# Block one's last pair first, low words on VectorE and MLP rows that run on, in a kernel of top-32 attention and two MLPs

## The chip, the cores and the metric

The kernel runs on one core of a Trainium2 chip. The metric is the device time of one execution in microseconds (us). A core has five engines with a queue of instructions each: TensorE (PE in the rows; PEld is its weight load), VectorE (DVE), ScalarE (ACT), GpSimd (POOL) and SyncE (SP), which here only issues DMAs.

## What is computed

q, k and v are 4 batches x 8 heads x 576 positions x 64, all float32. Each row of scores keeps its 32 largest entries; the rest is masked away before the softmax. The 4 x 576 = 2304 rows of the result (8 x 64 = 512 wide) go through two MLPs of 512 -> 2048 -> 512.

```python
scores = scale * np.matmul(q, k.transpose(0, 1, 3, 2))
kth = np.partition(scores, -32, axis=-1)[..., -32:-31]
scores = np.where(scores >= kth, scores, -1e9)
attn = softmax(scores)                   # sum + 1e-9
x = concat_heads(np.matmul(attn, v))     # 2304 x 512
h = np.maximum(x @ w_in, 0);  x = (h * h) @ w_out
h = x @ w2_in;  out = np.maximum(0.01 * h, h) @ w2_out
```

The MLPs' weights reach the chip as 64-bit floats and are turned there into two words each, a high and a low one, both in the matmul's reduced float32 format; the same is done with q, k, x and the hidden layer. A product then takes three matmuls (high by high, high by low, low by high).

## The kernel before

**Attention.** A tile is 128 rows of scores x 576 columns, of one pair of heads. Two tiles make a pair; there are 72 pairs. `UNITS` orders the rows: unit 0 and 1 are rows 0 to 511 of batch 0, unit 2 is rows 0 to 255 of batch 1, unit 3 the last 64 rows of batch 0, unit 4 the last 320 of batch 1, and units 5 to 8 are batches 2 and 3. For each unit the four head pairs come one after another. VectorE finds the 32 largest of a tile in four rounds: MAX8 gives the 8 largest, MATCH_REPLACE8 strikes them out (lines 867 and 869). Then, for a pair: `shifts` (L315, GpSimd) takes threshold minus maximum, `drop` (L321) and `expo_sum` (L325) are ScalarE's masking and exponential with the sum, `recip` (L329 on GpSimd, L330 on VectorE) the reciprocal, `pt_main` (L339) transposes on TensorE into a PSUM bank of the three called `att`. `pt_left` does the last 64 columns and transposes the reciprocal. For units 0 and 1 the transposed tile is kept as float32 (`PT`, L349), `av` (L425) multiplies by V and `x_out` scales by the reciprocal (`xn`, L456). For units from 2 on (`split`, tiles 32 and up) the exponentials are scaled beforehand (`norm`) and the transposed tile is split in two words: ScalarE copies the bank twice, once as the high word (`PTs`, L344) and once whole (`whole`, L346), and GpSimd subtracts (L347). `x_out` then writes the two words of x (`xh` L457, `xl` L460) into the buffers of the MLP.

**Scores ahead.** Batches 2 and 3 (`EARLY`) have their scores computed long before they are searched: `scores` (L303, L304) into `stage` and out to DRAM, read back later by `load_s`. These `fill` events lie in slots 2 to 245 (`FILL`). The unit called `KEPT` (unit 3) is treated so too, beside unit 1 whose K it shares.

**The MLPs.** x is cut in six blocks of 512, 256, 384, 512, 256 and 384 rows; units 0 and 1 are block one (index 0), unit 2 is block two, units 3 and 4 block three. A block goes through layer one in 16 steps of 128 hidden units (h matmuls L619, acc matmuls L656), then through layer two (L619, L656 and L658). The 32 steps of block one are the first use of the weights. For each, a DMA brings 1 MB of 64-bit words, `w_convert` makes the two-word weights (ScalarE L532 and L541, VectorE's bit operations L547 and L548, ScalarE's high part L552, GpSimd's subtraction L553) and `w_store` writes 1 MB to DRAM, from which later blocks load them. In the first step of a layer the chunks of x are taken in the order `OPENING`, so that it can start before the last head pair is there.

**What sets the order.** The program is written out in slots; pair p has slots 16p to 16p+15, one search operation each, and `at(slot, f)` puts everything else at a slot before or after (scores 30 before, shift 14 after the pair's first slot, transposes at 20, `av` at 30). `run_moe` emits MLP work between: per slot `rate` quanta of three matmuls. A block's rate is its quanta by the slots until the next block is ready (L824), and when a block becomes ready what is left of the one before is emitted at once (the `while active` under L875). A scheduler then orders each engine's queue by priority (order of writing, with attention 100 ahead, `SOON`) and by a model of times; `issue_after` pins an instruction behind another. Block one is ready at slot 274 (16 x 15 + 30 + 4, for its last pair is pair 15), block two at slot 402.

The lines that pace the MLP and convert the first two weight steps:

```python
rate.append(sum(quanta(*ph) for ph in groups[j]) / max(nxt - rslot[j] - 1, 40))   # L824
at(rslot[0] - 80, w_raw, 0)
at(rslot[0] - 28, convert_now, 0)
at(rslot[0] - 14, convert_now, 1)
```

Of the kernel before, what the change touches and what calls it, by code (L numbers as in the profile page):

```python
# [8 lines left out]
F = mybir.dt.float32  # L9
R = mybir.dt.float32r  # L10
U = mybir.dt.uint32
# [34 lines left out]

KEPT = 3

EARLY = (2, 3)
FILL = (2, 245)  # L50
KPB = 2
NST = 5
SDB = 2
SPB = 3

NS = 6
# [8 lines left out]

SOON = 100
SEAM = 400
CONVP = 30

# [17 lines left out]
def topk_attention_moe_moe2_kernel(  # L87
# [127 lines left out]
    def at(slot, fn, *a):  # L215
        events.setdefault(slot, []).append((fn, a))


    KT = {}
# [65 lines left out]
    def scores(t, half):  # L285
# [50 lines left out]
    def pt_main(t):  # L336
        ps = bank()
        for j in range(NJ):
            PE.transpose(ps[:, j * P:(j + 1) * P], t["e"][:, j * P:(j + 1) * P], ident)  # L339
        c = t["col"]  # L340
        x = ps.rearrange("p (j t) -> p j t", j=NJ)
        if split(t["uh"]):
            pts = late["PT"]
            ACT.activation(pts[:, 0:4, c:c + P], x, AF.Copy)  # L344
            whole = late["pool"].tile([P, NJ, P], F, tag="whole", name="whole", bufs=2)
            ACT.activation(whole, x, AF.Copy)  # L346
            POOL.tensor_tensor(pts[:, 4:8, c:c + P], whole, pts.bitcast(F)[:, 0:4, c:c + P], op=OP.subtract)  # L347
        else:
            ACT.activation(PT[:, 0:4, c:c + P], x, AF.Copy)  # L349
# [94 lines left out]
    def x_out(uh, hs):  # L444
# [13 lines left out]
        if m < n:  # L458
            ACT.activation(spill[r, hp, 0:n - m], x[r, m:n], AF.Copy)
        POOL.tensor_tensor(xl[r, c:c + m], x[r, 0:m], xh.bitcast(F)[r, c:c + m],  # L460
                                                   op=OP.subtract)
        if hp == NHP - 1 and hs[-1] == 1 and g0 + n >= end:
# [62 lines left out]
    def w_convert_steps(i):  # L525
# [30 lines left out]
        for todo in STAGES:  # L556
            for fn, x in todo:
                dict(high=high, bits=bits, parts=parts)[fn](x)
            yield 0

    def w_store(i):
# [206 lines left out]

    pairs = []
    for p in range(NPAIRS):  # L770
        pr = dict(t=tiles[2 * p:2 * p + 2], p=p)
        pairs.append(pr)
        z = 16 * p
        for i, t in enumerate(pr["t"]):
            if kept(t["uh"]):
# [25 lines left out]
    for uh in uhs:  # L801
        if split(uh):
# [6 lines left out]
            continue  # L809
        apart = uh["n"] > P and uh["n"] % P and uh["ti"] % 2 == 0  # L810
        for hs in ((0,), (1,)) if apart else ((0, 1),):
            z = 16 * (uh["lastA"] // 2 if hs == (0,) else uh["last"] // 2) + 30
            nq = 2 * len(hs)
            for i in range(nq):
                at(z + i, av, uh, hs, i)
            at(z + nq, x_out, uh, hs)
# [4 lines left out]
    rate = []  # L821
    for j, blk in enumerate(blocks):
        nxt = rslot[j + 1] if j + 1 < len(blocks) else rslot[j] + 40
        rate.append(sum(quanta(*ph) for ph in groups[j]) / max(nxt - rslot[j] - 1, 40))  # L824

    def convert_now(i):
        for _ in w_convert(i):
            pass

    at(rslot[0] - 80, w_raw, 0)  # L830
    at(rslot[0] - 80, w_raw, 1)
    at(rslot[0] - 28, convert_now, 0)
    at(rslot[0] - 27, w_raw, 2)
    at(rslot[0] - 14, convert_now, 1)
    at(rslot[0] - 13, w_raw, 3)
    at(rslot[0] - 10, w_store, 0)

# [3 lines left out]
    def run_moe(amount):  # L841
        while amount >= 1 and active:
            try:
                next(active[0])
                amount -= 1
            except StopIteration:
                active.pop(0)
        return amount
# [3 lines left out]
    while slot <= last:  # L852
# [20 lines left out]
        for fn, a in events.pop(slot, []):  # L873
            nr = len(ready)
            with tc.high_priority(offset=SOON):  # L875
                fn(*a)
            for blk in ready[nr:]:
                if not (len(ready) > nr + 1 and blk is ready[-1]):
                    while active:
                        run_moe(1)  # L880
                if blk["idx"] + 1 < len(blocks) and blocks[blk["idx"] + 1].get("spilled"):
                    unspill(blocks[blk["idx"] + 1])
                active.extend(moe(*ph) for ph in groups[blk["idx"]])
                credit = 0.0
                cur["rate"] = rate[blk["idx"]]
        if active:
# [56 lines left out]
```

## Time and profile before

| what | us |
|---|---|
| median of 3 runs (lowest, highest) | 1193.88 (1189.94, 1194.23) |
| the profiled execution | 1189.77 |
| its span, first to last instruction | 1188.0 |
| TensorE busy / VectorE / ScalarE / GpSimd | 1124.0 / 872.1 / 820.1 / 744.8 |
| a load of raw weights, 1 MB, issue to landing (32 of them) | 7.9 |
| a store of converted weights, 512 KB (64 of them) | 7.8 to 8.4 |

The profile is of one execution. Times in the rows are from the span's start. Busy times of the engines overlap, so they don't add up to the span. An engine's own idle time costs only where the end waits for it. The matmuls' ends are modelled, so the time from one matmul's start to the next is a better measure of pace than a single duration.

### The profile page before, as it was taken

Reading aid. Unit: us, or ns where it says so; the run is one execution under the profiler, and the core shown is the slowest. Engines: PE = TensorE matmul, PEld = TensorE weight load, DVE = VectorE, ACT = ScalarE, POOL = GpSimd, SP = SyncE. Lnnn points to the kernel's source line nnn. Section 1 sums busy time; section 2 is a strip of 40 time slices with the busy share of each in tenths; the row PEclk is TensorE's granted clock in tenths of the full one; section 3 lists DMA queues with packets and bytes.
Section 4 is the critical chain, followed back from the end, with each engine's and each line's share of the span. In section 5 each row is a group of like instructions: output and inputs, shape, how many; then the busy total and the mean of one; then the engine's idle time right before and its main releaser. Section 6 shows DMA issues by size and latency. Waiting matters only on the chain.

```text
span 1188.0 us, 20096 instructions
## 1 busy us (share of the span) xinstructions
PE 1124.0 (95%) x6376; PEld 985.5 (83%) x6376; DVE 872.1 (73%) x1828; ACT 820.1 (69%) x1823; POOL 744.8 (63%) x958
## 2 busy tenths in 40 slices
PE   5899977989899999999999999999999999999997
PEld 4777765868688899898998998788888899998996
DVE  7999999888886668999999999989997400110010
ACT  6999998899989667887676777556766743332322
POOL 7968846999879677677886775767665653002100
PEclk9999989999899999999999999999999999999999
DMA  9868756899999698799888888667776499779973
GB/s 307 287 216 276 264 187 230 312 334 333 394 353 360 199 336 293 240 346 371 312 264 296 286 283 287 217 219 219 232 234 215 151 326 334 256 252 351 346 258 119
DMA packets 108201, 329.53 MB, mean 277 GB/s; under 512 B 17216, under 2 KB 25408, under 8 KB 104000
## 3 DMA queue, kind: packets, MB, share of 16 engines
q1 hardware_dynamic: 105472, 323.53, 79.8%
q10 hardware_dynamic: 2624, 4.72, 1.1%
q8 instruction: 52, 0.85, 0.3%
q14 instruction: 53, 0.43, 0.1%
HBM read 257.03 MB, written 71.17 MB: 276 GB/s over the span
## 4 chain that ended last, share of the span: by engine, by line
PE 57%; DVE 21%; ACT 12%; DMA 5%; issue 2%; POOL 2%; ACTq 0%; SPq 0%; POOLq 0%; DVEq 0%
PE h L619 22%; PE acc L658 13%; DVE m L867 10%; PE acc L656 9%; DVE w L869 8%; PE att L425 3%; PE att L436 3%; PE att L339 3%; ACT e L321 2%; ACT stage L304 1%; PE sp L303 1%; ACT e L325 1%; DMA wraw<-in_w_dram 1%; DMA out_dram<-y 1%; ACT s L304 1%
## 5 line engine op out<-in xcount | busy, mean ns | idle before, releaser
L619 PE MATMUL h<-xh,wi 128*128 128x512 f32 (+2 forms) x1280 | 345.9, 344 | 9.7 <-ACT ga L629 4.5
L867 DVE MAX8 m<-w 128x8 f32<-128x576 f32 x432 | 315.1, 756 | 1.8
L619 PEld LDWEIGHTS h<-xh,wi 128*128 128x128 f32 x1280 | 225.4, 190 | 38.6 <-ACT ga L629 6.7
L639 POOL TENSOR_TENSOR gl<-ga,gh 128x512 fp32r<-128x512 f32 (+2 forms) x160 | 162.5, 1018 | 137.2 <-ACT gh L638 110.9
L869 DVE MATCH_REPLACE8 w<-m,w 128x576 f32<-128x576 f32 x288 | 215.2, 751 | 0.5
L619 PE MATMUL h<-xl,wi 128*128 128x512 f32 (+2 forms) x640 | 203.3, 338 | 0.0
L347 POOL TENSOR_TENSOR PTs<-whole,PTs 128x512 fp32r<-128x512 f32 x112 | 144.6, 1297 | 43.7 <-ACT whole L346 43.2
L656 PE MATMUL acc<-gh,wo 128*128 128x512 f32 (+2 forms) x768 | 156.5, 343 | 0.8 <-ACT y L674 0.5
L658 PE MATMUL acc<-wo,gh 128*128 128x512 f32 x576 | 152.1, 396 | 0.5 <-ACT gh L638 0.5
L656 PEld LDWEIGHTS acc<-gh,wo 128*128 128x128 f32 x768 | 127.4, 190 | 13.4 <-ACT y L674 0.7
L321 ACT ACTIVATE e<-s,m 128x576 f32<-128x576 f32 x144 | 112.9, 785 | 32.3 <-DVE m L867 27.4
L639 DVE TENSOR_TENSOR gl<-ga,gh 128x384 fp32r<-128x384 f32 x32 | 17.9, 559 | 152.1 <-ACT gh L638 149.4
L619 PEld LDWEIGHTS h<-xl,wi 128*128 128x128 f32 x640 | 120.0, 189 | 10.6
L636 ACT ACTIVATE ga<-h 128x512 f32<-128x512 f32 (+2 forms) x96 | 46.6, 491 | 116.3 <-PE h L619 114.8
L658 PEld LDWEIGHTS acc<-wo,gh 128*128 128x128 f32 x576 | 105.4, 188 | 21.2 <-ACT gh L638 0.9
L867 DVE MAX8 m<-s 128x8 f32<-128x576 f32 x144 | 104.3, 754 | 17.7 <-ACT s L304 15.2
L325 ACT ACTIVATE e<-e,nb 128x576 f32<-128x576 f32 x144 | 111.5, 782 | 1.8 <-POOL nb L315 1.7
L869 DVE MATCH_REPLACE8 w<-m,s 128x576 f32<-128x576 f32 x144 | 108.2, 752 | 0.6
L339 PE MATMUL att<-ident,e 128*128 128x128 f32 x576 | 90.1, 277 | 7.6 <-DVE wc L548 3.0
L334 POOL TENSOR_SCALAR e<-e,rc 128x576 f32<-128x576 f32 x112 | 82.5, 748 | 16.0 <-DVE rc L330 14.5
L656 PE MATMUL acc<-gl,wo 128*128 128x512 f32 (+2 forms) x384 | 88.3, 349 | 3.8 <-POOL gl L639 3.8
L631 POOL TENSOR_TENSOR ga<-ga 128x512 f32<-128x512 f32 (+2 forms) x80 | 66.3, 829 | 36.9 <-ACT gh L630 36.7
(90 smaller groups left out, 2117.4 us busy)
## 6 DMA issues: line engine op xcount, KB each, us to landing
wi<-wd SPq DMA_DIRECT2D x160, 512.0 KB, 5.1
wo<-wd SPq DMA_DIRECT2D x160, 512.0 KB, 5.0
wraw<-in_w_dram SPq DMA_DIRECT2D x32, 1024.0 KB, 7.9
sd<-stage SPq DMA_DIRECT2D x76, 288.0 KB, 3.3
s<-sd SPq DMA_DIRECT2D x76, 288.0 KB, 4.8
wd<-wi SPq DMA_DIRECT2D x32, 512.0 KB, 7.8
wd<-wo SPq DMA_DIRECT2D x32, 512.0 KB, 8.4
vd<-VT SPq DMA_DIRECT2D x16, 640.0 KB, 5.8
```

The lines of the kernel that those rows point to most:

```text
L321: ACT.activation(t["e"], t["s"], AF.Prelu, bias=pr["m8"][:, i, 31:32], scale=-1.0, alpha=1.0 / FAR)
L325: ACT.activation(e, e, AF.Exp, bias=pr["nb"][:, i:i + 1], scale=-FAR, accum_out=pr["sum"][:, i:i + 1])
L334: POOL.tensor_scalar(e, e, pr["rc"][:, i:i + 1], 1.0, op0=OP.mult, op1=OP.mult)
L339: PE.transpose(ps[:, j * P:(j + 1) * P], t["e"][:, j * P:(j + 1) * P], ident)
L347: POOL.tensor_tensor(pts[:, 4:8, c:c + P], whole, pts.bitcast(F)[:, 0:4, c:c + P], op=OP.subtract)
L619: PE.matmul(two[r][:, 0:n], lhsT=ws[r][:, w, c * P:(c + 1) * P], rhs=x[c][y][:, 0:n], start=cnt == mine[0], stop=cnt == mine[-1])
L631: POOL.tensor_tensor(a[:, 0:n], a[:, 0:n], a[:, 0:n], op=OP.mult)
L639: (DVE if j >= GLD else POOL).tensor_tensor(gl[:, 0:n], a[:, 0:n], gh.bitcast(F)[:, 0:n], op=OP.subtract)
L656: PE.matmul(acc[c][:, 0:n], lhsT=wo[:, w, cs], rhs=g[:, 0:n], start=first, stop=last)
L658: PE.matmul(acc[c], lhsT=g[:, cs], rhs=wo[:, w, :], start=first, stop=last)
L867: cur["dve"] = DVE.max(out=m8[:, x, 8 * r:8 * r + 8], in_=t["s"] if r == 0 else t["w"])
L869: cur["dve"] = DVE.match_replace(out=t["w"], in_to_replace=m8[:, x, 8 * r:8 * r + 8], in_values=t["s"] if r == 0 else t["w"], imm_value=NEG)
```

## The change

Pair 15, the last of block one (`first_done`), gets a chain of its own: its shift moves from GpSimd to VectorE, the sum's small term to ScalarE, the last subtraction of x to VectorE; all its steps from the shift to `x_out` are written at slots 13 to 17 after its first one instead of 14 to 34, with a priority of 800 ahead (`URGENT`), and the product with V of its last head pair is done by head, the first head's at slot 251. Block one is so marked ready at slot 257.

The first two weight steps are converted by functions of their own: `lead_passes` (ScalarE, into the PSUM banks of the scores ahead, slots 224 and 230) and `lead_bits` (VectorE behind the shift and the reciprocal; the high part on GpSimd instead of ScalarE). Loads, splits and the scores from pair 17 on that stood in slots 236 to 256 move to slot 257.

The scores ahead end at slot 222. Tiles 32 to 51 have their low word subtracted on VectorE straight from the bank, without `whole`. The 64-row unit of batch 0 comes behind the 320-row unit of batch 1, and `KEPT` follows it. The MLP's rate is what is still to do by the slots to the next block plus 24 (`LATE`), and what is left then runs on; only before x's buffer is taken over is it emitted at once.

```diff
-    (0, 0, 256), (0, 256, 256), (1, 0, 256), (0, 512, 64), (1, 256, 320),
+    (0, 0, 256), (0, 256, 256), (1, 0, 256), (1, 256, 320), (0, 512, 64),
-KEPT = 3
+KEPT = 4
-FILL = (2, 245)
+FILL = (2, 222)
+LOW_D = 52
+LATE = 24
+URGENT = 800
...
-        elif uh["b"] == 0:
+        elif t["i"] // 2 <= first_done + 1 or kept(uh):
             ps = stage_psum.tile([P, 512], F, tag="sd", name="sd", bufs=SDB)
...
-        POOL.tensor_tensor(t, pr["m8"][:, :, 31], pr["m8"][:, :, 0], op=OP.subtract)
+        on = DVE if pr["p"] == first_done else POOL
+        cur["shift"] = on.tensor_tensor(t, pr["m8"][:, :, 31], pr["m8"][:, :, 0], op=OP.subtract)
...
-        POOL.tensor_scalar(pr["sum"], pr["sum"], 1e-9, 1.0, op0=OP.add, op1=OP.mult)
-        DVE.reciprocal(pr["rc"], pr["sum"])
+        if pr["p"] == first_done:
+            ACT.activation(pr["sum"], pr["sum"], AF.Copy, bias=1e-9)
+        else:
+            POOL.tensor_scalar(pr["sum"], pr["sum"], 1e-9, 1.0, op0=OP.add, op1=OP.mult)
+        cur["recip"] = DVE.reciprocal(pr["rc"], pr["sum"])
...
-            whole = late["pool"].tile([P, NJ, P], F, tag="whole", name="whole", bufs=2)
-            ACT.activation(whole, x, AF.Copy)
-            POOL.tensor_tensor(pts[:, 4:8, c:c + P], whole, pts.bitcast(F)[:, 0:4, c:c + P], op=OP.subtract)
+            if t["i"] < LOW_D:
+                DVE.tensor_tensor(pts[:, 4:8, c:c + P], x, pts.bitcast(F)[:, 0:4, c:c + P], op=OP.subtract)
+            else:
+                whole = late["pool"].tile([P, NJ, P], F, tag="whole", name="whole", bufs=2)
+                ACT.activation(whole, x, AF.Copy)
+                POOL.tensor_tensor(pts[:, 4:8, c:c + P], whole, pts.bitcast(F)[:, 0:4, c:c + P], op=OP.subtract)
...
+    def lead_passes(i):
...
+            ACT.activation(b, lo, AF.Copy, scale=L_SCALE, bias=L_BIAS)
+            ACT.activation(v, hi.bitcast(F), AF.Copy, scale=H_SCALE)
+    def lead_bits(i):
+        for b, vu, w in led.pop(i):
+            with behind("recip" if i else "shift"):
+                DVE.scalar_tensor_tensor(b, vu, 3, b, op0=OP.logical_shift_left, op1=OP.bitwise_or)
+                DVE.scalar_tensor_tensor(b, vu, 0x80000000, b, op0=OP.bitwise_and, op1=OP.bitwise_or)
+            split_hi(w[:, 0, :], b.bitcast(F))
+            POOL.tensor_tensor(w[:, 1, :], b.bitcast(F), w.bitcast(F)[:, 0, :], op=OP.subtract)
...
+        if p == first_done:
+            at(z + 13, urgent(shifts), pr)
+            for i in range(2):
+                at(z + 13, urgent(drop), pr, i)
+                at(z + 13, urgent(expo_sum), pr, i)
+            at(z + 13, urgent(recip), pr)
+            for i in range(2):
+                at(z + 14, urgent(pt_main), pr["t"][i])
+            at(z + 14, urgent(pt_left), pr)
+            continue
...
-        apart = uh["n"] > P and uh["n"] % P and uh["ti"] % 2 == 0
+        tight = uh["last"] // 2 == first_done
+        apart = uh["n"] > P and (uh["n"] % P or tight) and uh["ti"] % 2 == 0
...
+            if fn is x_out and "x" not in blocks[cur["fill"]]:
+                shared = [x for x in range(cur["fill"]) if SETS[x] == SETS[cur["fill"]]]
+                while any(x[2] in shared for x in active):
+                    run_moe(1)
...
-                if not (len(ready) > nr + 1 and blk is ready[-1]):
-                    while active:
-                        run_moe(1)
...
+                todo = sum(x[1] for x in active)
+                cur["rate"] = todo / (rslot[j + 1] - slot + LATE if j + 1 < len(blocks) else 40)
```

## Rows read from the trace of the kernel before

**Rows 1.** The page: busy time by engine, and the chain that ended last
```profile
PE 1124.0 (95%) x6376; PEld 985.5 (83%) x6376; DVE 872.1 (73%) x1828; ACT 820.1 (69%) x1823; POOL 744.8 (63%) x958
...
PE 57%; DVE 21%; ACT 12%; DMA 5%; issue 2%; POOL 2%; ACTq 0%; SPq 0%; POOLq 0%; DVEq 0%
```

**Rows 2.** Busy us (instructions) by stretch: length, engines, granted clock, DMA share, GB/s
```profile
20.00:150.00 130.00, 117.96 (x695) 97.58 (x694) 128.41 (x280) 122.64 (x344) 104.56 (x158) 0.99 0.79 266
174.00:191.20 17.20, 14.34 (x58) 9.33 (x56) 17.13 (x37) 15.13 (x33) 6.26 (x9) 0.93 0.59 202
191.20:320.00 128.80, 114.64 (x514) 91.04 (x514) 112.43 (x214) 116.56 (x222) 118.70 (x122) 0.95 0.93 329
320.00:411.00 91.00, 90.99 (x435) 75.17 (x436) 65.95 (x125) 76.04 (x138) 69.63 (x67) 1.00 0.87 315
411.00:551.00 140.00, 138.16 (x1030) 130.93 (x1029) 124.73 (x273) 105.11 (x265) 100.27 (x143) 1.00 0.88 311
551.00:731.00 180.00, 175.11 (x1043) 163.29 (x1042) 178.39 (x385) 131.64 (x282) 139.52 (x183) 1.00 0.87 294
943.00:1188.00 245.00, 236.98 (x1455) 223.60 (x1453) 23.56 (x45) 81.54 (x178) 42.63 (x57) 0.99 0.80 276
```

**Rows 3.** Timeline 168 to 192 us: start, length, instruction, [idle before and releaser]
```profile
168.54 1.29 DVE L547 SCALAR_TENSOR_TENSOR wc<-att,wc 128x512 uint32<-128x512 uint32 x2
...
171.11 1.30 DVE L548 SCALAR_TENSOR_TENSOR wc<-att,wc 128x512 uint32<-128x512 uint32 x2
...
173.03 1.43 DVE L867 MAX8 m<-w 128x8 f32<-128x576 f32 x2
...
176.19 0.19 POOL L315 TENSOR_TENSOR nb<-m 128x2 f32<-128x2 f32 x1
...
178.46 0.79 ACT L325 ACTIVATE e<-e,nb 128x576 f32<-128x576 f32 x1
...
181.75 0.16 DVE L330 RECIPROCAL rc<-sum 128x2 f32<-128x2 f32 x1
...
183.80 3.79 PE L425 MATMUL att<-PT,VN 128*128 128x256 f32 x15
...
190.06 0.42 DVE L456 TENSOR_TENSOR xn<-att,rb 128x256 f32<-128x256 f32 x1
...
190.78 0.41 ACT L457 ACTIVATE xh<-xn 128x256 fp32r<-128x256 f32 x1
...
191.24 1.19 PE L619 MATMUL h<-xh,wi 128*128 128x512 f32 x4 [0.17 <-ACT xh L457]
```

**Rows 4.** GpSimd by line, 150 to 215 us: count, busy us, mean ns, idle before
```profile
L553 POOL TENSOR_TENSOR wi<-wc,wi 128x512 fp32r<-128x512 f32 x4 | 5.2, 1288 | 3.8 <-ACT wi L552 2.9 <-PE att L303 0.8
```

**Rows 5.** ScalarE by line, 20 to 150 us
```profile
L304 ACT ACTIVATE stage<-sp 128x288 f32<-128x288 f32 x126 | 47.3, 444 | 1.7 <-DMA sd<-stage 1.0 <-PE sp L303 0.3
```

**Rows 6.** ScalarE, GpSimd and VectorE by line, 215 to 410 us
```profile
L346 ACT ACTIVATE whole<-att 128x512 f32<-128x512 f32 x14 | 8.4, 599 | 0.0
...
L347 POOL TENSOR_TENSOR PTs<-whole,PTs 128x512 fp32r<-128x512 f32 x14 | 18.3, 1308 | 3.8 <-ACT whole L346 3.8
...
L671 DVE TENSOR_TENSOR xl<-acc,xh 128x512 fp32r<-128x512 f32 x4 | 2.6, 680 | 0.0
```

**Rows 7.** A wait for GpSimd, the clock behind it, and eight like matmuls later
```profile
204.65 2.07 PE L656 MATMUL acc<-gl,wo 128*128 128x512 f32 x4 [2.72 <-POOL gl L639]
...
206.52 3.62 PE L656 MATMUL acc<-gh,wo 128*128 128x512 f32 x8
...
204.00:208.00 4.00, 3.35 (x8) 2.67 (x9) 4.00 (x7) 4.00 (x12) 4.00 (x5) 0.50 0.71 240
...
290.22 2.03 PE L656 MATMUL acc<-gh,wo 128*128 128x512 f32 x8
```

**Rows 8.** Timeline: transposes that waited for a bank held by VectorE's bit operations
```profile
195.19 0.63 PE L339 MATMUL att<-ident,e 128*128 128x128 f32 x4 [1.42 <-DVE wc L548]
...
306.53 1.08 PE L339 MATMUL att<-ident,e 128*128 128x128 f32 x4 [1.58 <-DVE wc L548]
```

More of the change, by code (lines that the diff above doesn't have):

```diff
@@ L216, in at, with urgent, run @@
         events.setdefault(slot, []).append((fn, a))
+    def urgent(fn):
+        def run(*a):
+            with tc.high_priority(offset=URGENT):
+                fn(*a)
+        return run
     KT = {}
@@ L559, in w_convert_steps @@
             yield 0
+    led = {}
+    def lead_passes(i):
+        led[i] = []
+        raw = wraw.pop(i)
+        c = pool.tile([P, 1024], U, tag="wc", name="wc", bufs=WCB)
+        for x, w in enumerate(w_alloc(i)):
+            xs = slice(x * 512, x * 512 + 512)
+            lo, hi, b = raw[:, xs, 0], raw[:, xs, 1], c[:, xs]
+            v = stage_psum.tile([P, 512], F, tag="sd" if len(led) == 2 and not led[i] else "sp", name="v",
+                                bufs=SDB if len(led) == 2 and not led[i] else SPB)
+            ACT.activation(b, lo, AF.Copy, scale=L_SCALE, bias=L_BIAS)
+            ACT.activation(v, hi.bitcast(F), AF.Copy, scale=H_SCALE)
+            led[i].append((b, v.bitcast(U), w))
+    def lead_bits(i):
[5 more added lines that the diff above has]
+            POOL.tensor_tensor(w[:, 1, :], b.bitcast(F), w.bitcast(F)[:, 0, :], op=OP.subtract)
     def w_store(i):
@@ L769, in topk_attention_moe_moe2_kernel @@
     pairs = []
+    first_done = next(uh["last"] // 2 for uh in uhs if uh["hp"] == NHP - 1 and uh["u"]["g0"] + uh["n"] >= BLOCKS[0])
     for p in range(NPAIRS):
@@ L773, in topk_attention_moe_moe2_kernel @@
         z = 16 * p
+        if p == first_done:
+            assert all(direct(t["uh"]) and not split(t["uh"]) for t in pr["t"])
+            for i, t in enumerate(pr["t"]):
+                at(z - DLEAD + 5 * i, scores, t, 0)
+                at(z - DLEAD + 2 + 5 * i, scores, t, 1)
+            at(z + 13, urgent(shifts), pr)
[7 more added lines that the diff above has]
+            continue
         for i, t in enumerate(pr["t"]):
@@ L820, in topk_attention_moe_moe2_kernel @@
         rmark(uh, z)
[L821 to L824, printed above, removed]
     def convert_now(i):
@@ L828, in convert_now @@
             pass
[L830 to L836, printed above, removed]
+    for i, z in enumerate((224, 230)):
+        at(z - 40, w_raw, i)
+        at(z, lead_passes, i)
+        at(16 * first_done + 13, lead_bits, i)
+        at(rslot[0] - 30 + i, w_raw, i + 2)
+    at(rslot[0] - 1, w_store, 0)
+    moved = []
+    for z in range(236, 256 + 1):
+        for fn, a in events.pop(z, []):
+            wait = fn in (load_k, load_q, load_v, split_k, split_q, split_v, request)
+            wait = wait or fn is scores and a[0]["i"] // 2 > first_done + 1
+            if wait:
+                moved.append((fn, a))
+            else:
+                events.setdefault(z, []).append((fn, a))
+    events[256 + 1] = moved + events.get(256 + 1, [])
     active = []
@@ L843, in run_moe @@
             try:
-                next(active[0])
+                next(active[0][0])
+                active[0][1] = max(active[0][1] - 1, 0)
                 amount -= 1
@@ L877, in topk_attention_moe_moe2_kernel @@
             for blk in ready[nr:]:
-                if not (len(ready) > nr + 1 and blk is ready[-1]):
-                    while active:
-                        run_moe(1)
[L881 to L885, printed above, removed]
+                j = blk["idx"]
+                if j + 1 < len(blocks) and blocks[j + 1].get("spilled"):
+                    unspill(blocks[j + 1])
+                active.extend([moe(*ph), quanta(*ph), ph[0]] for ph in groups[j])
+                todo = sum(x[1] for x in active)
+                cur["rate"] = todo / (rslot[j + 1] - slot + LATE if j + 1 < len(blocks) else 40)
         if active:
```

11 lines of the change are left out of this document (6 added, 5 removed).

## The prediction

> **What bounds the kernel now.** I read the page first: TensorE is busy for 1124.0 of 1188.0 us, and the chain that ended last lies 57% on it and 21% on VectorE [rows 1]. A mean over the span hides where the rest is, so the second view is the busy time by stretch [rows 2]. The reader is to see four different limits in it. From 20 to 150 us VectorE is the bound (128.41 of 130): it searches the tiles of block one, and ScalarE beside it is nearly full too (122.64). From 174 to 191 us block one's last pair is on its way from the search to the MLP. From 191 to 320 us nobody is idle and nobody is full: ScalarE 116.56, GpSimd 118.70, VectorE 112.43 of 128.8, TensorE 114.64 with 14.2 us idle. From 320 on TensorE is full (90.99 of 91, then 138.16 of 140; in the last 245 us 236.98, and most of what is missing there is the wait for the last output). Between 551 and 731 us VectorE is full as well (178.39 of 180) and TensorE lacks 4.9 us.
>
> So a microsecond of TensorE idle that goes before 731 us is a microsecond off the end, since the MLP's matmuls behind it only move up. The change can win in three places: the hand-over at 174 to 191 us, the 14.2 us of 191 to 320, and the 1.8 and 4.9 us of 411 to 731.
>
> The third view is the timeline of the hand-over [rows 3]. The last MAX8 of pair fifteen is the first of the two at 173.03, so the search ends at about 173.8. Before it, in the same queue, stand four bit operations of the weights' conversion (1.29 + 1.30 us). After it: GpSimd's `nb` at 176.19 (the engine was in a weight subtraction), the last exponential at 178.46, the reciprocal only at 181.75 (in VectorE's queue), the product with V from 183.80 on (15 of its 20 records took 3.79 us), `xn` at 190.06 (again in VectorE's queue), and the first matmul on the last chunk of x at 191.24. That is 17.4 us from search to MLP, of which the operations themselves are less than half.
>
> **The change part by part.**
>
> *The chain of pair fifteen (urgent, shift on VectorE, sum on ScalarE, half of the product).* The bit operations move behind the shift: the search ends 2.6 us earlier, at 171.2. From there: shift 0.2; exponential of the first tile, drop and exponential of the second with their accumulator reads 2.8 (from 0.79 each, 0.2 per read [rows 3]); last four transposes 0.63, as in [rows 8]; their copy 0.6, as a copy of that shape in [rows 6]; the product with V for head one alone, ten instead of twenty matmul records, 2.5; `xn` 0.42; `xh` 0.4; and eight hand-overs between engines at about 0.2 as between the rows of the timeline, 1.5. That is 9.1 us, so the last chunk would be ready at 180.3 instead of 191.2: 10.9 us earlier. Matmuls that ran in that gap have to be done in any case, and the scores of pair seventeen, put off to slot 257, come out of it, so I take 9. Bounds: nothing, if the queues stay as they are (VectorE's and ScalarE's above all); 11, if all of it comes through.
>
> *The first two weight steps.* Their ScalarE conversions move ahead into slots 224 and 230, their eight bit operations behind the shift and the reciprocal, and their high parts from ScalarE to GpSimd. Behind the shift that is 2.6 us of VectorE per step, and on GpSimd four high parts and four subtractions of 1.29 us each [rows 4]; the high parts I put at half to all of a subtraction. Step one's input weights are ready near 175.5 and step two's near 179 by that: both ahead of the last chunk of x, which hides them. Cost nothing; if GpSimd takes the order badly, up to two subtractions, 2.6 us. What is late next is pair sixteen's search, 5 us behind bits and reciprocal; nothing of the end hangs on it, as block two is ready long after.
>
> *Scores ahead (the fill) in slots 2 to 222 instead of 245.* The same copies of 0.444 us [rows 5] in 220 slots for 243: 47.3 us in that stretch become 52.2, while ScalarE has 7.4 us left of 130 [rows 2]. It fits, but ScalarE then feeds VectorE's search with 2 us in hand. Bounds 0 and +5; I take +1.5. In return ScalarE and TensorE are free of it when the chain runs; that is in the 9 us.
>
> *Low words of tiles 32 to 51 on VectorE.* Off ScalarE go 20 copies of 0.599 us (12.0 us), off GpSimd 20 subtractions of 1.308 us (26.2 us), onto VectorE come 20 subtractions out of PSUM. The nearest row is the same form, L671, 0.68 us: 13.6 us [rows 6]. All of it lies between 190 and 420 us, where VectorE has 41 us left, ScalarE 27, GpSimd 31. Where TensorE stood in that stretch, GpSimd was late: at 204.65 it had waited 2.72 us for `gl`, and the eight matmuls begun at 206.52 took 3.62 us, where eight of the same kind at 290.22 took 2.03: the granted clock was 0.50, the lower of the two levels (1.2 GHz), after that wait [rows 7]. So the idle is both in waits and in the slow time behind them. I take 8 of the 14.2 us; bounds all 14.2 plus what the clock lost (a mean of 0.95 over 128.8 us [rows 2], 6.4), 21, and on the other side a loss, the second rival.
>
> *Rate (24 slots more, no flush).* Block one's 256 quanta are spread over 402 - 257 + 24 = 169 slots instead of 127: 1.51 a slot for 2.02. Attention gets ahead in 190 to 411 us, and block one's rest fills the hand-over to block two. What it can win is the 1.8 and 4.9 us idle of 411 to 731 [rows 2]; nothing is computed less. I take 2, bounds -6.7 and +3 (attention in front costs ScalarE and GpSimd more per matmul than MLP does, in the stretch where both are short).
>
> *Order of units, KEPT, slots 236 to 256 held back.* The 64-row unit moves behind the 320-row one; the same tiles, loads and matmuls, 4 conversions of V later. Slots 236 to 256 put loads and pair seventeen's scores at most 21 slots later, about 13 us, while VectorE still has pair sixteen. Nothing, within 2 us.
>
> Sum: -9 + 0 + 1.5 - 8 - 2 + 0 = -17.5 us. The profiled execution took 1189.77 us; the sum gives 1172.3 for it. The median of the runs shown is 1193.88, 4.1 us above that execution, so I predict 1176.4, say 1176.
>
> A rule speaks against the fill's earlier end. By the Trainium skill, page "TensorE: Matmul & The Clock Gate", Part 1, the array's default is the half clock and only its own activity releases the full one. With the fill gone from about 150 us on, the clock would by that rule fall ahead of the chain and not only beside it, and its transposes and products would run at 1.2 GHz; priced by the low stretch of [rows 7] that is up to 3.4 us, and the sum would be -14.1. The trace agrees that the clock is low behind idle time ([rows 7]); it doesn't show which stretch the change would lose, and I leave the sum as it is.
>
> **The rivals.** *More comes through (0.20).* The chain gives 11, the freed engines all 21 of the stretch to 320, the spread rows 5: 1.5 - 37 gives about -35, 1158. For it: the idle time is shown, and each piece has a cause that the change touches. Against: ScalarE keeps 90% of its load there, so waits only get shorter.
>
> *The low words hold a bank (0.12, slower).* Until VectorE has subtracted, a transposed tile's PSUM bank stays taken, and there are three for transposes, scores and products alike. VectorE's queue is strict, with searches of 0.75 us in it. Where a bank hung on VectorE before (the conversion's bits), TensorE's transposes waited 1.42 and 1.58 us [rows 8], MLP matmuls queued behind them. Twenty tiles at 1.5 us are 30 us: -9 + 1.5 - 2 + 30 = +20 with no relief left, 1214; with the relief of 8 left, 1206. It decides from 0.9 us of mean wait per tile on, where the 17.5 us are used up. Against: ScalarE's second copy held the same bank 0.6 us before, and VectorE is less full there (178 of 220).
>
> *The time goes back to the stretch (0.15, no change).* DMA is at 0.93 in 191 to 320 us [rows 2], each fresh weight step moves 2 MB (one in, one out), and ScalarE is at 90%. If these pace block one's two layers, an earlier start only makes each step wait, and the fill's 1.5 and the other bounds take the rest: 1190. For it the DMA share; against it that from 320 to 411 the same steps run with TensorE full at 0.87.
>
> **How the numbers follow.** The forecast, faster by 10 to 26 us (1168 to 1184), has 0.53, the rivals 0.20, 0.15 and 0.12. A measurement of this kernel can tell about 0.5%, 6 us, from no change: faster is below 1187.9, slower above 1199.9. Forecast and the first rival are both faster, 0.73; same 0.15; slower 0.12. The range from 1156 to 1196 takes in the forecast with the bounds of its terms, most of the first rival and the unchanged time, and leaves out the held bank and the far end of the gain.
>
> **What would show it.** Right: pair fifteen's `xh` near 180 instead of 190.78; no bit operation between its last searches; reciprocal within 1 us of the exponentials; TensorE's idle between 191 and 320 below 8 us; 20 subtractions on VectorE of about 0.7 us; block two's x before 411 us. Wrong: VectorE idle before 170 us (the fill), transposes that wait for VectorE's low words (the bank), or the two layers of block one as long as before with DMA at 1.0. The forecast fails if the end of the last search of pair fifteen comes later than 175 us, or if more than 10 us of new waits of TensorE on VectorE stand between 190 and 420.

## The result and the profile after: 1% slower

The changed kernel takes 1205.67 us (median of 4, 1203.25 to 1207.52) against 1192.68 for the kernel before on the same chip: a ratio of 1.011, interval 1.0082 to 1.0138. The forecast was 1176, faster. The profiled execution took 1205.85 us, its span is 1203.7: 15.7 us more than before. In the table of the experiments, one execution of `a_late` that ran at a granted clock of 0.56 and took 1830.34 us is left out.

Busy time by engine and the shares of the chain, from the page after; beside [rows 1] the reader sees 8.7 us more of TensorE busy for the same 6376 matmuls (the other 7.0 us of the longer span are idle time), and a chain that hardly touches VectorE any more (4% for 21%):

```profile
PE 1132.7 (94%) x6376; PEld 989.4 (82%) x6376; DVE 884.3 (73%) x1851; ACT 807.8 (67%) x1795; POOL 723.7 (60%) x948
...
PE 57%; DVE 4%; DMA 3%; ACT 2%; POOL 1%; issue 1%; SPq 0%; ACTq 0%; POOLq 0%
```

Busy time by stretch, the same stretches and columns as [rows 2] (the last one is longer by 16 us):

```profile
20.00:150.00 130.00, 117.84 (x684) 96.45 (x683) 129.04 (x280) 120.30 (x332) 104.68 (x164) 0.97 0.78 266
...
174.00:191.20 17.20, 14.96 (x63) 11.11 (x64) 13.76 (x28) 12.00 (x28) 9.91 (x13) 0.90 0.43 177
191.20:320.00 128.80, 117.18 (x525) 91.21 (x523) 117.28 (x225) 109.36 (x212) 100.62 (x104) 0.96 0.89 304
320.00:411.00 91.00, 86.36 (x414) 69.84 (x414) 75.90 (x144) 77.88 (x146) 58.97 (x59) 1.00 0.83 293
411.00:551.00 140.00, 134.68 (x981) 126.39 (x979) 134.75 (x291) 103.98 (x251) 100.40 (x142) 1.00 0.92 317
551.00:731.00 180.00, 173.36 (x1047) 163.75 (x1047) 175.51 (x381) 130.13 (x285) 143.22 (x190) 0.98 0.86 299
...
943.00:1204.00 261.00, 252.00 (x1511) 234.90 (x1509) 23.06 (x44) 81.64 (x176) 41.68 (x55) 0.99 0.78 271
```

TensorE's idle time (the length of a stretch less its busy time) fell from 14.2 to 11.6 us between 191 and 320 us. From 320 to 411 it rose from 0 to 4.6, from 411 to 551 from 1.8 to 5.3, from 551 to 731 from 4.9 to 6.6. No engine is full in the stretch where TensorE lost 4.6 us (VectorE 75.9, ScalarE 77.9, GpSimd 59.0 of 91).

Busy time hides slow pace, so I also added up, matmul by matmul, the time from one start to the next beyond the usual pace of its size (232 ns at 512 columns, 174 at 384, 117 at 256, 133 for scores, 108 for transposes, 216 for block one's products). Their difference, 15.5 us, is the whole of the 15.7 us by which the span grew:

| us beyond pace, until | first MLP matmul | block one, layer one | layer two | block two | block three | block four | rest | sum |
|---|---|---|---|---|---|---|---|---|
| before | 50.6 | 27.4 | 2.9 | 5.5 | 9.0 | 5.4 | 4.3 | 105.1 |
| after | 55.1 | 23.5 | 10.0 | 8.9 | 13.3 | 4.0 | 5.8 | 120.6 |

The gain of 3.9 us in block one's first layer is there; 4.5 us are lost ahead of it, 7.1 in its second layer, and 7.7 in blocks two and three.

**The hand-over.** The timeline of the changed kernel from the last search of pair 15 to the first matmul on the last chunk of x:

```profile
168.80 0.76 DVE L930 MAX8 m<-w 128x8 f32<-128x576 f32 x1
...
171.31 0.14 DVE L326 TENSOR_TENSOR nb<-m 128x2 f32<-128x2 f32 x1
...
174.01 3.47 PE L442 MATMUL att<-PT,VN 128*128 128x256 f32 x8 [1.67 <-ACT PT L366]
...
175.12 0.80 ACT L336 ACTIVATE e<-e,nb 128x576 f32<-128x576 f32 x1
...
176.81 0.15 DVE L344 RECIPROCAL rc<-sum 128x2 f32<-128x2 f32 x1
...
178.31 0.60 PE L353 MATMUL att<-ident,e 128*128 128x128 f32 x4
...
179.25 0.66 PE L353 MATMUL att<-ident,e 128*128 128x128 f32 x4
...
180.37 1.38 PE L659 MATMUL h<-xh,wi 128*128 128x512 f32 x5 [0.23 <-ACT s L314]
...
184.08 1.89 PE L442 MATMUL att<-PT,VN 128*128 128x256 f32 x8
...
186.66 0.43 PE L392 MATMUL att<-ident,rc 128*128 128x128 f32 x2
...
188.33 0.38 ACT L407 ACTIVATE rb<-att 64x256 f32<-64x256 f32 x1
188.73 0.41 ACT L314 ACTIVATE s<-att 128x288 f32<-128x288 f32 x1
188.76 1.23 PE L313 MATMUL att<-KT,q 128*128 128x288 f32 x6 [1.53 <-ACT rb L407]
188.81 0.43 DVE L473 TENSOR_TENSOR xn<-att,rb 64x256 f32<-64x256 f32 x1 [2.13 <-ACT rb L407]
...
190.38 1.83 PE L659 MATMUL h<-xh,wi 128*128 128x512 f32 x4 [0.39 <-ACT xh L474]
```

The search ends at 169.6, the reciprocal comes 0.9 us behind the last exponential, and yet the first matmul on the last chunk is at 190.38 against 191.24 [rows 3]: 20.8 us instead of 17.4 behind a search that ends earlier. The time went into TensorE's queue. The transposes at 178.31 and 179.25 stood behind the first head's product (174.01 to 177.5, mostly at the low clock: a granted clock of 0.62 from 174 to 178 us, and 8 records in 3.47 us, where 8 at 184.08 took 1.89). The second head's product stood behind MLP matmuls from 180.37 to 184.1, and the transposed reciprocal behind the product. Its copy (188.33) stood in ScalarE's queue behind the masking and exponential of the next pair. So the priority of 800 did not bring the links together: in the trace each of them ran behind what the scheduler had put ahead of it in its engine's queue.

### The profile page after: what moved, and what is told of

Read it like the earlier page. It is cut to its first block, busy times and chain, and to the rows that moved or that the text cites. A ratio compares the mean times of both kernels' runs of the same rounds, so it can differ in the third digit from the quotient of the medians.

```text
span 1203.7 us, 20101 instructions
## 1 busy us (share of the span) xinstructions
PE 1132.7 (94%) x6376; PEld 989.4 (82%) x6376; DVE 884.3 (73%) x1851; ACT 807.8 (67%) x1795; POOL 723.7 (60%) x948
## 4 chain that ended last, share of the span: by engine, by line
PE 57%; DVE 4%; DMA 3%; ACT 2%; POOL 1%; issue 1%; SPq 0%; ACTq 0%; POOLq 0%
PE h L659 25%; PE acc L698 13%; PE acc L696 10%; PE att L453 4%; PE att L353 3%; DVE m L930 2%; DVE w L932 1%; DMA wi<-wd 1%; DMA vraw<-in_v_dram 1%; PE att L371 1%; DMA out_dram<-y 1%; PE att L313 0%; POOL PTs L364 0%; ACT e L332 0%; ACT PTs L358 0%
## 5 line engine op out<-in xcount | busy, mean ns | idle before, releaser
L659 PE MATMUL h<-xl,wi 128*128 128x512 f32 (+2 forms) x640 | 206.2, 341 | 0.0
L364 POOL TENSOR_TENSOR PTs<-whole,PTs 128x512 fp32r<-128x512 f32 x92 | 118.5, 1294 | 38.5 <-ACT whole L363 38.5
L698 PEld LDWEIGHTS acc<-wo,gh 128*128 128x128 f32 x576 | 105.5, 188 | 21.5 <-ACT gh L678 0.8
L332 ACT ACTIVATE e<-s,m 128x576 f32<-128x576 f32 x144 | 111.2, 779 | 13.3 <-PE att L371 7.5
L930 DVE MAX8 m<-s 128x8 f32<-128x576 f32 x144 | 105.1, 752 | 14.0 <-ACT s L314 10.8
L453 PE MATMUL att<-PTs,VT 128*128 128x256 f32 (+2 forms) x504 | 86.7, 300 | 6.6 <-DVE wc L565 2.7
```

The source lines that it names most:

```text
L332: ACT.activation(t["e"], t["s"], AF.Prelu, bias=pr["m8"][:, i, 31:32], scale=-1.0, alpha=1.0 / FAR)
L453: PE.matmul(ps, lhsT=l, rhs=r, start=i == 0, stop=i == len(mm) - 1)
L659: PE.matmul(two[r][:, 0:n], lhsT=ws[r][:, w, c * P:(c + 1) * P], rhs=x[c][y][:, 0:n], start=cnt == mine[0], stop=cnt == mine[-1])
L698: PE.matmul(acc[c], lhsT=g[:, cs], rhs=wo[:, w, :], start=first, stop=last)
L930: cur["dve"] = DVE.max(out=m8[:, x, 8 * r:8 * r + 8], in_=t["s"] if r == 0 else t["w"])
```

## The experiments

All ratios are to the kernel before on the same chip, with 95% intervals. The names say the starting point: u_ undoes one part of the changed kernel, b_ puts one part into the kernel before, a_ rewrites the changed kernel. The kernel before has medians of 1191.3 to 1192.7 us in its measurements beside these runs.

| kernel | median us | ratio |
|---|---|---|
| after | 1205.67 | 1.0110 (1.0082 to 1.0138) |
| u_order / u_low | 1204.35 / 1201.31 | 1.0112 (1.0096 to 1.0128) / 1.0092 (1.0075 to 1.0109) |
| u_rate / u_chain | 1203.46 / 1203.40 | 1.0120 (1.0084 to 1.0157) / 1.0110 (1.0080 to 1.0139) |
| b_fill / b_chain | 1190.90 / 1192.97 | 0.9995 (0.9980 to 1.0011) / 1.0016 (1.0003 to 1.0028) |
| b_low / b_low46 | 1203.04 / 1194.83 | 1.0084 (1.0056 to 1.0112) / 1.0031 (1.0014 to 1.0049) |
| b_order / b_rate | 1209.28 / 1210.04 | 1.0150 (1.0133 to 1.0166) / 1.0142 (1.0116 to 1.0168) |
| b_order_rate | 1206.34 | 1.0121 (1.0102 to 1.0140) |
| b_r1 / b_r3 | 1186.62 / 1200.81 | 0.9953 (0.9927 to 0.9979) / 1.0073 (1.0049 to 1.0098) |
| b_rm3 / b_one | 1196.53 / 1201.19 | 1.0045 (1.0029 to 1.0060) / 1.0082 (1.0053 to 1.0112) |
| a_late / a_late25 | 1206.83 / 1209.01 | 1.0124 (1.0100 to 1.0148) / 1.0145 (1.0124 to 1.0165) |
| a_low51 | 1208.74 | 1.0144 (1.0102 to 1.0186) |

**One part undone.** Each from the changed kernel.

```diff
# u_order
-UNITS = [... (1, 256, 320), (0, 512, 64), ...]; KEPT = 4
+UNITS = [... (0, 512, 64), (1, 256, 320), ...]; KEPT = 3
# u_low
-LOW_D = 52
+LOW_D = 0
# u_rate
-cur["rate"] = todo / (rslot[j + 1] - slot + LATE ...)
+while active: run_moe(1)
+cur["rate"] = quanta of block j / max(nxt - rslot[j] - 1, 40)
# u_chain: pair 15, weight steps 0 and 1 and slots 236 to 256 as before
```

u_order: 

> The changed kernel with only the order of units and KEPT put back (the 64-row unit of batch 0 third again, its scores from DRAM). Theory 'scores of the next unit land in block one's second layer': pairs 24 to 27 then need no or fewer direct scores there, the waits of products and scores for a bank go, 1196 to 1200 us. Theory 'low words hold the bank': no gain, 1203 to 1208. Theory 'attention in front is what costs': no gain, 1203 to 1208.

u_low: 

> The changed kernel with the low words of tiles 32 to 51 back on ScalarE's second copy and GpSimd. Theory 'low words hold the bank' (and lengthen VectorE's queue): most of the 13 us comes back, 1193 to 1198. The other theories: 1205 to 1212, since ScalarE gets 12 us and GpSimd 26 us more in the full stretch.

u_rate: 

> The changed kernel with the MLP's pace of before: quanta by the slots to the next block, and the rest emitted at once when a block is ready. Theory 'attention in front is what costs': block one's second layer no longer stretches (111 us to under 100) and 1194 to 1198. The other theories: 1203 to 1208, since TensorE's work is the same.

u_chain: 

> The changed kernel with pair 15's chain, the first two weight steps and slots 236 to 256 as before (block one ready at slot 274 again). Theory 'the chain is what costs' (the queues put other work ahead of it and the rest is displaced): 1193 to 1198. The others: 1204 to 1208, since the chain moved the first matmul on the last chunk by under 1 us.

None of the four theories holds: every one of the parts can be taken out and 10 to 13 us of loss stay. u_low is nearest to a gain, and its interval overlaps the changed kernel's. In u_rate block one's second layer was to take less than 100 us again; it takes 109.4, so the pace is not what stretches it.

**One part alone.** Each from the kernel before, the same edits the other way round; b_chain has the chain, the weight steps, the held slots and the fill.

b_fill: 

> The kernel before with one part of the change alone: the scores ahead end at slot 222 instead of 245. Theory 'the fill is what costs', the part not yet undone in the changed kernel: 1198 to 1205 (ScalarE has 7 us left of 130 and TensorE loses its spare work before the hand-over). Theory 'no part alone, any new order of the queues': 1195 to 1203 here as well as in the three others. Theory 'only several parts together': 1189 to 1194.

b_low: 

> The kernel before with the low words of tiles 32 to 51 on VectorE alone. Theory 'low words hold the bank': 1195 to 1201. Theory of the prediction, ScalarE and GpSimd relieved: 1180 to 1188. Theory 'any new order of the queues': 1195 to 1203. Theory 'only several parts together': 1188 to 1193.

b_order: 

> The kernel before with the order of units and KEPT changed alone. Theory 'direct scores land in the second layer of block one': 1195 to 1200. Theory 'any new order of the queues': 1195 to 1203. Theory 'only several parts together': 1189 to 1194.

b_rate: 

> The kernel before with the MLP's pace alone: 24 slots more and the rest running on. Theory of the prediction: 1188 to 1192. Theory 'attention in front is what costs': 1195 to 1202, block one's second layer longer than 96 us. Theory 'any new order of the queues': 1195 to 1203. Theory 'only several parts together': 1189 to 1194.

b_chain: 

> The kernel before with the chain of pair 15, the first two weight steps, slots 236 to 256 and the earlier fill; the order of units, the low words and the MLP's pace as before. Theory of the prediction, 9 us off: 1182 to 1186. Theory 'any new order of the queues costs': 1196 to 1206. Theory 'the chain itself is not run first': the last chunk's first matmul within 2 us of 191, 1190 to 1196.

The fill costs nothing, the chain with it 0.2%. Low words, order and pace cost 0.8, 1.5 and 1.4% alone. The sum of the parts is 3.9%, the changed kernel has 1.1%: they don't add. b_order and b_rate lie above every range that was expected of them.

The time beyond pace, summed as above, shows where each part loses (b_fill's trace is of an execution 6 us above its median):

| us beyond pace, until | first MLP matmul | block one, layer one | layer two | block two | block three | block four | rest | sum |
|---|---|---|---|---|---|---|---|---|
| before | 50.6 | 27.4 | 2.9 | 5.5 | 9.0 | 5.4 | 4.3 | 105.1 |
| b_fill | 54.1 | 32.0 | 4.8 | 5.4 | 4.1 | 7.5 | 5.2 | 113.1 |
| b_chain | 58.2 | 21.5 | 8.1 | 5.1 | 9.2 | 2.6 | 4.8 | 109.4 |
| b_low | 50.7 | 18.8 | 10.1 | 9.0 | 10.9 | 11.2 | 7.8 | 118.4 |
| b_order | 54.4 | 27.6 | 3.4 | 9.4 | 15.2 | 6.6 | 9.7 | 126.2 |
| b_rate | 51.8 | 34.0 | 3.8 | 13.8 | 5.3 | 10.9 | 7.5 | 127.0 |
| u_chain | 55.5 | 27.0 | 5.3 | 11.5 | 8.7 | 4.2 | 7.1 | 119.2 |
| u_rate | 58.6 | 16.4 | 8.9 | 10.2 | 15.1 | 3.9 | 6.3 | 119.4 |

The two parts that speed up block one's first layer, chain and low words, give most of it back in the second: 5.9 us gained and 5.2 lost in b_chain, 8.6 and 7.2 in b_low. What makes b_low slower than the kernel before lies mostly behind that, in blocks two to four and the rest, though only four of its 20 low words start after block two does.

In b_low the first step came true, and was given back at once. Its stretches from 191 us on, columns as above:

```profile
191.20:320.00 128.80, 120.81 (x554) 96.50 (x554) 115.58 (x220) 111.73 (x209) 111.08 (x114) 0.97 0.92 329
320.00:411.00 91.00, 85.55 (x398) 69.58 (x397) 71.36 (x134) 72.04 (x131) 56.95 (x57) 0.98 0.90 321
```

TensorE's idle falls by 6.2 us up to 320 (14.2 to 8.0) and rises by 5.4 up to 411. Layer two of block one starts at 301.3 instead of 311.5 us and block two at 411.2 instead of 410.9. Of the 5.4 us, 5.1 are two waits of TensorE for ScalarE's `gh` in layer two; ahead of the second, ScalarE itself had waited for raw weights. The timeline of b_low, TensorE and then ScalarE:

```profile
345.92 3.63 PE L662 MATMUL acc<-wo,gh 128*128 128x512 f32 x8 [2.27 <-ACT gh L642]
...
360.79 2.13 PE L662 MATMUL acc<-wo,gh 128*128 128x512 f32 x8 [2.86 <-ACT gh L642]
```
```profile
357.28 0.63 ACT L545 ACTIVATE att<-wraw 128x512 f32<-128x512 f32 x1 [1.17 <-DMA wraw<-in_w_dram]
...
360.13 0.61 ACT L642 ACTIVATE gh<-ga 128x512 fp32r<-128x512 f32 x1
```

**Low words in layer one only.**

```diff
# b_low46
-LOW_D = 52
+LOW_D = 46
```

> The kernel before with the low words on VectorE only for tiles 32 to 45, those whose transposes fall in block one's first layer. Theory 'low words help in layer one, where GpSimd squares as well, and cost in layer two, where VectorE is the late one': layer one ends as early as with all 20 (301 us, 10 us before the unchanged kernel), layer two takes 100 instead of 110 us, 1181 to 1187. Theory 'any new order': 1195 to 1206.

A miss: layer two starts early again (302.7 us) and block two at 414.5; 0.3% slower. The edit didn't do what it was meant to: the 14 low words run from 200.0 to 373.7 us, so some lie in layer two still. Whether low words there stretch it stays untold; six fewer don't shorten it (111.8 for 109.9 us).

**Changes with no purpose.** If the parts have no price that adds up, perhaps any rewriting of the queues has one.

```diff
# b_r1, b_r3, b_rm3: the rate of the kernel before
-max(nxt - rslot[j] - 1, 40)
+max(nxt - rslot[j], 40)        # b_r1; + 2 in b_r3, - 4 in b_rm3
# b_one: b_low for one tile of 112
-if t["i"] < LOW_D:
+if t["i"] == 32:
```

b_r3: 

> The kernel before with its MLP rate divided by three slots more (130 for 127 before block two), a change of 2% with no purpose, which writes the queues in another order from about the 630th of TensorE's 3017 instruction groups on. Theory 'any new order of the queues costs, before is a good draw': 1196 to 1206. Theory 'each part has its own price': 1190 to 1194.

b_one: 

> The kernel before with one low word of 112 (tile 32, the first) on VectorE: 0.7 us of work moved, all queues behind it written anew. Theory 'a new order of the queues is what costs': 1195 to 1206. Theory 'each part has its own price': 1190 to 1193.

b_rm3: 

> The kernel before with its MLP rate from three slots fewer (124 for 127 before block two), no purpose, other queues from about 190 us on. Theory 'a new order': 1195 to 1206, with low clock or idle of TensorE at other block hand-overs than 170, 204 and 306. Theory 'a lower rate costs, a higher one gains' (the three slots more cost 9 us): 1183 to 1190.

b_r1: 

> The kernel before with its MLP rate from one slot more (128 for 127), no purpose, the same queues up to a later point than with three. Theory 'a new order': 1194 to 1204. Theory 'a lower rate costs' in proportion: 1193 to 1196.

One tile on VectorE, 0.7 us of work, costs 9.6 us; twenty cost 11.4. The rate off by +1, +3 and -3 slots gives -5.0, +9.5 and +4.9 us: no sign that follows the rate, and b_r1 lies below both of its ranges. So a change of at most a few us of work moves this kernel between -0.5 and +0.8%, through the order in which the queues are written. The idle of TensorE shows it. The stretches 411 to 731 us of b_r1, b_one and b_order in turn:

```profile
411.00:551.00 140.00, 136.76 (x1006) 129.93 (x1005) 121.87 (x266) 105.54 (x261) 95.66 (x137) 0.98 0.86 299
551.00:731.00 180.00, 177.75 (x1059) 166.24 (x1058) 178.36 (x384) 128.24 (x280) 140.25 (x185) 1.00 0.87 300
```
```profile
411.00:551.00 140.00, 137.14 (x1017) 129.53 (x1016) 117.91 (x259) 104.28 (x262) 97.81 (x140) 1.00 0.86 295
551.00:731.00 180.00, 174.76 (x1045) 163.38 (x1045) 178.31 (x386) 129.79 (x282) 142.12 (x186) 1.00 0.87 299
```
```profile
411.00:551.00 140.00, 136.49 (x1004) 128.36 (x1003) 133.77 (x286) 105.48 (x256) 101.04 (x145) 1.00 0.86 304
551.00:731.00 180.00, 170.47 (x1020) 158.82 (x1019) 176.64 (x384) 130.24 (x282) 143.07 (x190) 0.99 0.86 294
```

TensorE idles there 5.5, 8.1 and 13.0 us, the kernel before 6.7 [rows 2]. Over 191 to 731 us the idle is 18.7 us in b_r1 (span 1184.8), 20.9 before (1188.0), 26.8 in b_one (1202.7), 28.2 after (1203.7), 28.4 in b_rate (1210.1) and 30.0 in b_order (1209.1): the longer of these kernels idle more, each in places of its own. It is a tendency and no rule: b_low (1201.0) idles 22.7 us there and u_order (1204.7) 33.7.

**The two dearest together, and the changed kernel rewritten without purpose.**

```diff
# b_order_rate: b_order and b_rate
# a_late, a_late25, a_low51: the changed kernel with one of
-LATE = 24
+LATE = 22        # a_late25: 25
-LOW_D = 52
+LOW_D = 51
```

b_order_rate: 

> The kernel before with both parts that cost most alone, the order of units (+18) and the MLP's pace (+18). Theory 'each part has its own price': 1224 to 1230. Theory 'a new order': 1198 to 1210, no more than either alone.

a_late: 

> The changed kernel with LATE at 22 instead of 24, a change with no purpose that also writes the queues anew. Theory 'any new order of the queues': anywhere from 1196 to 1212, as far from the changed kernel as the single parts are from each other. Theory 'each part has its own price': 1203 to 1207.

a_low51: 

> The changed kernel with one low word of its 20 (tile 51) back on GpSimd: 0.7 us of work moved, queues behind it written anew from about 400 us on. Theory 'each part has its own price': 1205 to 1207. Theory 'the order of the queues': 1196 to 1212, off by more than the 1 us that one tile could be worth.

a_late25: 

> The changed kernel with LATE at 25 instead of 24, no purpose. Theory 'each part has its own price': 1205 to 1207. Theory 'the order of the queues': 1196 to 1212. If it stays within 2 us, as with LATE at 22, the changed kernel lies on a level of its own, and not only its order is slow.

Order and pace together cost 1.2%, less than either alone. The changed kernel's rewritings lie at 1.2 to 1.5%, 2 to 4 us above it by ratio, with intervals that overlap its own. Those of the kernel before lie at -0.5 to +0.8%. So both things are true of the orders that were run: a rewriting scatters by about half a per cent either way, and the changed kernel lies on a level some 1% higher (mean of its four orders 1.3%; of b_fill, b_r1, b_r3, b_rm3 and b_one 0.3%). The sums beyond pace tell where: three traces of the one (after, a_late25, a_low51) lie 11 us above five of the other (before, b_r1, b_r3, b_rm3, b_one) in the mean, 4.5 us of it ahead of the first MLP matmul and 7.3 in blocks two and three.

## Why the prediction was wrong

**The step that failed** is the premise under the terms: "a microsecond of TensorE idle that goes before 731 us is a microsecond off the end". Idle time did go between 191 and 320 us, 2.5 us here and 6.2 in b_low, and the end did not move up: the time beyond pace fell by 3.9 us in block one's first layer and rose by 19.4 in all other places together. The first rival, more of the same gains, rests on this premise too. Neither of the two signs of failure that I had named came: the last search of pair fifteen ended at 169.6 us (175 was the bound), and TensorE's waits on VectorE from 191 to 420 us are 5.3 us for 4.7 before (10 new ones were the bound).

**The chain, -9 us: failed.** The last chunk of x came 0.9 us earlier, the first MLP matmul 6 us later (180.4 for 174.1), and the time beyond pace up to it grew by 4.5 us. My 9.1 us were the operations and eight hand-overs; the chain took 20.8, because in each engine's queue other work stood between its links. I had named that bound ("nothing, if the queues stay as they are") and took the other end. [rows 2] has a closer bound that I passed over: TensorE was busy for 14.34 of the 17.20 us of the hand-over, so no more than 2.9 us of idle time stood there; MLP matmuls on the first chunks ran in the gap. Alone, with the fill (b_chain, +0.2%), the links do run closer together (8.1 us from the reciprocal to the last `xh`, for 13.1 in the changed kernel), and these matmuls stand behind them. TensorE's timeline in b_chain:

```profile
183.05 2.62 PE L442 MATMUL att<-PT,VN 128*128 128x256 f32 x10 [1.10 <-ACT PT L366]
...
186.14 1.32 PE L659 MATMUL h<-xh,wi 128*128 128x512 f32 x5
...
190.61 1.08 PE L659 MATMUL h<-xh,wi 128*128 128x512 f32 x4
```

The last `xh` starts at 187.0 instead of 190.8 us there, the first MLP matmul at 186.14 instead of 174.12, and the first on the last chunk at 190.61 instead of 191.24: nothing is won. Nor are the 4.5 us ahead of the first MLP matmul the chain's alone: with the chain undone (u_chain) they stay (55.5 us beyond pace).

**The first weight steps at nothing: failed in the timeline.** They were to be hidden by the first chunks' matmuls, but those need them. Step one's low part ended at 176.5 (GpSimd's subtraction of 1.27 us from 175.24; estimated 175.5), and by then TensorE's queue had the transposes and scores of the chain in front, to 180.4.

**The fill, +1.5: a miss on the safe side.** ScalarE is busy 120.3 of 130, VectorE 129.04, and b_fill is unchanged. By the Trainium skill ("TensorE: Matmul & The Clock Gate", Part 1) the clock falls without activity. The trace agrees: the granted clock is 0.68 from 168 to 174 us, where TensorE is busy for 2.7 of 6 us, and the product at 174.01 took 3.47 us for 8 records. But the kernel before was low at that place too (0.72 from 168 to 172 us and 0.50 from 172 to 176), so it is little of the difference.

**Low words, -8: right in kind and place, and not kept.** 20 subtractions of 682 ns (estimated 680) came, and 2.5 us of idle went from 191 to 320. GpSimd then waited instead: ahead of its weight subtraction it stood idle for 28.2 us until ScalarE's high part came, where it was 1.3 us before. By line from 215 to 410 us, before and after:

```profile
L553 POOL TENSOR_TENSOR wi<-wc,wi 128x512 fp32r<-128x512 f32 x28 | 36.6, 1306 | 1.5 <-ACT wi L552 1.3
```
```profile
L570 POOL TENSOR_TENSOR wi<-wc,wi 128x512 fp32r<-128x512 f32 x26 | 33.7, 1296 | 33.2 <-ACT wi L569 28.2 <-issue 3.4 <-PE h L659 1.6
```

GpSimd's idle time costs nothing by itself; it shows that GpSimd was not what the stretch hung on any more. Where I went wrong is the step from "this idle goes" to "the end moves": b_low shows it coming back within 90 us, as waits of TensorE for ScalarE's `gh`.

**The held bank (rival, 1206 to 1214): the number by luck, not the mechanism.** In the changed kernel TensorE waited 0.2 us in all for a bank held by a low word; the first block is the low words and what waited for them, the second TensorE's longest waits from 191 to 420 us:

```profile
L360 DVE TENSOR_TENSOR PTs<-att,PTs x20: 672/682/685, 221.3 to 425.1; 128x512 fp32r<-128x512 f32 x20
...
  PE att L313: 0.2, 1
```
```profile
PE att L453 <- DVE wc L565: 2.7, 4, 1.2
PE acc L696 <- ACT gh L670: 2.5, 2, 1.6
PE att L313 <- ACT s L314: 1.6, 2, 1.0
```

The first of these is the same kind of bank, held by the conversion's bits as in [rows 8], four times 0.7 us: VectorE is busier from 320 to 411 us (75.9 for 65.95 us). Each of the others has another cause; none is the 7 us of layer two. In b_low the mechanism does appear, in small: scores waited twice, 2.9 us in all, for a bank that a low word held.

**The pace, -2 (bounds -6.7 and +3): sign and bound failed.** Attention did get ahead: the last `xh` of block two ends at 402.6 instead of 411.7 us. But the idle from 411 to 731 us rose by 5.2 us, and the pace alone measured +1.4%: b_rate loses 6.6 us in block one's first layer and 8.3 in block two. Block one's layer two, 112.2 instead of 99.4 us (first h matmul to block two's first), is not the pace's doing: it takes 109.4 with the pace undone (u_rate), 104.7 with the pace alone (b_rate) and 109.9 with the low words alone (b_low). The order of units, at nothing within 2 us, measured +1.5% alone. Both lie above the four rewritings without purpose, which are too few to make a price of it; that they don't add, and that undoing either changes nothing, the runs show but don't explain.

**The time goes back to the stretch (rival, no change): in part, and not by the transfers.** The DMA share fell to 0.89 and 0.83 where it was 0.93 and 0.87, and a load of raw weights took 6.4 us from issue to landing for 7.9 (medians). Still ScalarE waited 8.5 us for raw weights where it had waited 0.9. Its waits for them from 191 to 425 us, before and after:

```profile
ACT att L541 <- DMA wraw<-in_w_dram: 0.7, 3, 0.3
ACT wc L532 <- DMA wraw<-in_w_dram: 0.2, 1, 0.2
```
```profile
ACT wc L549 <- DMA wraw<-in_w_dram: 8.5, 6, 3.0
```

The loads took less time and yet came late for ScalarE, so they were issued late. They stand in SyncE's queue with the stores of the converted weights, and these waited for GpSimd's subtractions; SyncE's waits for the input weights' subtractions in the same stretch, before and after:

```profile
SPq L566 <- POOL wi L553: 33.6, 20, 4.1
```
```profile
SPq L606 <- POOL wi L570: 64.8, 21, 4.8
```

So it looks as if load, bits, high part, subtraction and store wait for one another in a ring, and an earlier start only makes each step wait, as the rival had it. The gain and loss of b_chain and b_low in the two layers fit that picture; how much of the 7.1 us of layer two is due to it no run separates.

One place of the later loss, for the kind of it. The timeline of the changed kernel, TensorE and then GpSimd, in the hand-over from layer one to two of block three:

```profile
647.06 0.38 PE L453 MATMUL att<-PTs,VT 128*128 128x256 f32 x1 [0.27 <-ACT whole L363]
650.13 0.96 PE L696 MATMUL acc<-gl,wo 128*128 128x384 f32 x4 [2.68 <-POOL gl L679]
650.93 2.28 PE L696 MATMUL acc<-gh,wo 128*128 128x384 f32 x8
```
```profile
647.07 0.83 POOL L671 TENSOR_TENSOR ga<-ga 128x384 f32<-128x384 f32 x1
647.85 1.27 POOL L364 TENSOR_TENSOR PTs<-whole,PTs 128x512 fp32r<-128x512 f32 x1
649.08 0.99 POOL L679 TENSOR_TENSOR gl<-ga,gh 128x384 fp32r<-128x384 f32 x1
```

A low word of attention stands ahead of the `gl` that TensorE waits for, 2.68 us; the granted clock is then 0.62 from 650.9 to 653.3 us, and 8 matmuls of 384 columns take 2.28 us, where 8 at 655.50 took 1.55. In the kernel before this hand-over, 633.8 to 642.1 us, lost less: 8.3 us from the last h matmul to the next layer's first against 14.7 (645.6 to 660.3).

**What stays open.** Why order and pace each lift the kernel by about 1%, and why not twice. No single wait stands out in all of the slow kernels; their idle lies in different hand-overs. A run with both undone and the rest kept, chain and low words, was not made.

## What to carry to other kernels

Where a scheduler writes the queues of five nearly full engines, estimate a rewriting first: make two or three changes without purpose and take their scatter (here -0.5 to +0.8%) as the width below which a part's price can't be read from one build. A priority shortens a chain only if what stands ahead of its links in each queue moves; sum the chain from the queue's order, not from its durations, and take no more from it than the time in which the engine that the end waits for stands idle there (2.9 of the 17.2 us here). And a stretch in which nothing is full does not gain what its idle time suggests: the relief of one engine there came back as waits for another within 90 us (b_low). The one build faster than both kernels is b_r1, 0.5%, by a rate off by one slot; that is a draw of the order and not a finding on the rate, since three slots more cost 0.7%.

## What the runs showed of the hardware

In the changed kernel the granted clock was 0.62 from 650.9 to 653.3 us, behind a wait of TensorE of 2.68 us, and eight matmuls of 384 columns took 2.28 us there and 1.55 at 655.50.

The mean granted clock of the span does not rank the kernels: it is 0.984 in b_r1, the fastest, 0.988 in the kernel before and 0.980 in b_r3, where it was low early (0.91 from 191 to 320 us). Executions of the kernel before alone lie between 0.984 and 0.991.

The subtraction of a low word, 128x512 out of PSUM, took 682 ns on VectorE (20 of them, 672 to 685). On GpSimd it took 1.31 us, behind a copy of 0.60 us on ScalarE [rows 6].
